# Token-major keys from matmuls, and two groups' queries on the two column halves of one bank

## The chip, the cores and the metric

The kernel runs on one core of one Trainium2 chip. The metric is the device time of one execution in microseconds (us); lower is better. The core has a matrix engine (TensorE; PE in the profile, with its weight loads as PEld), a vector engine (VectorE, DVE), a scalar engine (ScalarE, ACT), GpSimd (POOL) and SyncE (SP), which here only issues DMAs. Each engine works through its own list of instructions in order. Matmuls write to PSUM, a small memory in banks of 512 fp32 values a partition; the other engines read the results from there.

## The reference

Two stages follow each other for a batch of 8 sequences of 3200 tokens with 256 features:

```python
scores = (1.0 / S) * np.matmul(z, z.transpose(0, 2, 1))      # z: 8 x 3200 x 64
attn   = np.maximum(scores, 0.0) ** 2
x      = u * np.matmul(attn, v)                               # u, v: 8 x 3200 x 256
wq, wk = x @ w_q, x @ w_k                                     # 256 -> 64
W_tok  = (1.0 / np.sqrt(64)) * np.einsum('bsd,btd->bst', wq, wk)
mixed  = np.einsum('bst,btd->bsd', W_tok, x)
out    = np.maximum(mixed, 0.0) @ w_out                       # 256 -> 256
```

The second stage has no nonlinearity between `W_tok` and `x`, so the kernel never forms `W_tok`: it computes the 64x256 matrix wk^T x, here called the heads, and then wq times that.

## The kernel before, in words

**Tiling.** A sequence has 25 tiles of 128 tokens. Output tokens are worked on in seven groups: six of four tiles (512 tokens) and one of a single tile. For a group, the scores of a token tile against the group's tokens are a 64x512 matmul (line 291), whose contraction has only 64 rows. Two such matmuls go to the two 64-row halves of the array ("lanes") and run side by side. The first stage (lines 303 and 305, on ACT or DVE) takes relu and a scale from PSUM to SBUF, the second (lines 314 and 316, on ACT or POOL) squares to fp16, tile `at`. The second product (line 448) multiplies `at` with `v` into two accumulators of a bank each, `acc0` and `acc1`, also in two lanes of 64 rows: a first pass does one bank with rows 0 to 63 and the other with rows 64 to 127, a second pass swaps them (`first_pass`, line 385; `second_pass`, line 396; a wait in `swap_after`, line 427, stands between).

**Turned blocks.** The score matrix is symmetric. For some pairs of groups (`is_turned`, line 221) the block of one is not computed again: its `at` tile is transposed by a DMA into a `tt` tile (line 335) and used for the other group. Ten of the fifteen pairs of wide groups are turned.

**The second stage.** When a group is complete its accumulators are multiplied by `u` into `x` (`gate`, line 472), and a DMA transposes `x` to `xT` (line 502). `keys_and_heads` (line 797) then issues the projections: a matmul with stationary weights [w_q w_k] of 128 columns and moving `xT`, 512 tokens wide, gives queries and keys at once, features on partitions (line 508). ACT copies them to SBUF (line 528), and a DMA transposes the keys half to token-major (`turn_keys`, line 530, DMA at 535). The heads matmuls (line 545) of an earlier group stand in the other bank of the same PSUM tile. At the end of a batch the heads are turned on TensorE by two matmuls with all 128 rows (line 594); `mix` (line 636) multiplies them with the queries, `mix_out` takes relu, and `project` (line 788) multiplies with w_out and writes the result.

**Order.** The instruction order is fixed by the Python program: a loop of steps `k`, each with six score tiles (four with a mix), one stretch of the second product, and at most one extra piece of the second stage: keys ("k"), mix ("m") or projection ("p"). Which piece comes is decided by due times (`between`, `mix_due`, `key_due`) and, for some steps, by a table `chosen` (line 895). The two lanes of such a piece are balanced by the columns that their matmuls stream, and the items of both lanes are emitted in order of their place in the lane (`Streams`, line 368). The last batch's tail is a list written by hand (`ENDING`, line 82). SP issues the `tt`, `xT` and key transposes, the `u` loads and the output stores, in order; POOL issues the loads of `v` and `z`.

Of the kernel before, what the change touches and what calls it, by code (L numbers as in the profile page):

```python
# [16 lines left out]
def kernel(  # L17
# [15 lines left out]
    P = 128  # L33
# [23 lines left out]
    pk = ctx.enter_context(tc.tile_pool(name="pk", bufs=1))  # L57
# [7 lines left out]
    pq = ctx.enter_context(tc.tile_pool(name="pq", bufs=11))  # L65
# [24 lines left out]
    zT, vs, us, xs, xTs, qks, ks, hacc, hss, rts, zds = ({} for _ in range(11))  # L90
# [91 lines left out]
    wqk = consts.tile([P, ND, 2, dh], FP16, tag="wqk", name="wqk")  # L182
    wkq = consts.tile([P, ND, 2, dh], FP16, tag="wkq", name="wkq")
    hz = [consts.tile([P, D], FP16, tag=f"hz{i}", name=f"hz{i}") for i in range(2)]
    wq2 = consts.tile([P, ND, 2, dh], FP16, tag="wq2", name="wq2")
    wk2 = consts.tile([P, ND, 2, dh], FP32, tag="wk2", name="wk2")
    wo = consts.tile([P, ND, D], FP16, tag="wo", name="wo")
    zeros = consts.tile([P, P], FP16, tag="zeros", name="zeros")
    kxs = [pk.tile([P, 4, 2, dh], FP16, tag=f"kx{i}", name=f"kx{i}") for i in range(4)]
# [16 lines left out]
    def cast_weights():  # L206
        nc.gpsimd.tensor_copy(out=wqk[:, :, 0, :], in_=raw["q"])
        nc.gpsimd.tensor_copy(out=wqk[:, :, 1, :], in_=raw["k"])
        nc.gpsimd.tensor_copy(out=wkq[:, :, 1, :], in_=raw["q"])
        nc.gpsimd.tensor_copy(out=wkq[:, :, 0, :], in_=raw["k"])  # L210

    def double_weights(half):
        nc.gpsimd.tensor_copy(out=wq2[:, :, half, :], in_=raw["q"])
        nc.gpsimd.tensor_copy(out=wk2[:, :, half, :], in_=raw["k"])
# [5 lines left out]

    def is_turned(gi, gj):
        return gi < gj < LASTG and (gj <= gi + FAR or (gi, gj) == (0, 4))
# [46 lines left out]
    tt_of, tt_free = {}, [(-1.0, n) for n in range(7)]  # L269
# [77 lines left out]
    class Item:  # L347
# [4 lines left out]
        def emit(self, rows, start, stop):  # L352
            return nc.tensor.matmul(  # L353
                out=self.out, lhsT=self.lhsT(rows), rhs=self.rhs(rows), start=start, stop=stop
            )

# [151 lines left out]
    def projections(b, gi, w, out, start=True, n0=0, n1=None):  # L508

        n1 = widths[gi] // P if n1 is None else n1  # L510
        return [
            Item(
                out=out,
                lhsT=lambda r, ac=ac: w[r, ac, :, :].rearrange("p t h -> p (t h)"),
                rhs=lambda r, ac=ac: xTs[b, gi][r, n0:n1, ac, :],
                start=(start and ac == 0),
                stop=(ac == ND - 1),
            )
            for ac in range(ND)
        ]  # L520

    def projections_out(b, gi, out):
        gw = widths[gi]
        if gi < LASTG:
            qks[b, gi] = pq.tile([P, W], FP16, tag="qk", name="qk")
        else:
            qks[b, gi] = pq.tile([P, P], FP16, tag="ql", name="ql", bufs=2)
        nc.scalar.copy(out=qks[b, gi][:, 0:gw], in_=out)  # L528

    def turn_keys(b, gi):  # L530
        gw = widths[gi]
        mine = slice(0, dh) if swapped(gi) else slice(dh, P)
        kxs.append(kxs.pop(0))
        ks[b, gi] = kxs[-1]
        nc.sync.dma_start_transpose(
            out=ks[b, gi][:, 0 : gw // P, 0, :],
            in_=qks[b, gi][mine, 0:gw],
        )

    def swapped(gi):  # L540
        return gi % 2 == 1 or gi == LASTG

    def heads(b, gis, ps, stop=True):

        parts = [(gi, n) for gi in gis for n in range(widths[gi] // P)]
        if b < last:
            return [
                Item(  # L550
                    out=ps[:, 1, ds(P + cc * dh, dh)],
                    lhsT=lambda r, gi=gi, n=n, cc=cc: xs[b, gi][r, n, ds(cc * P, P)],
                    rhs=lambda r, gi=gi, n=n: ks[b, gi][r, n, 0, :],
# [8 lines left out]
                out=ps[:, 1, 0:D],  # L562
                lhsT=lambda r, gi=gi, n=n: ks[b, gi][r, n, :, :].rearrange("p a h -> p (a h)"),
# [7 lines left out]
    def heads_out(b, gis, ps):  # L571
        cols, n = (P, ND * dh) if b < last else (dh, D)
        part = ps[:, 1, P : P + n] if b < last else ps[0:dh, 1, 0:D]
        if gis[0] == 0:
            hacc[b] = psml.tile([P, n], FP32, tag="hT" if b < last else "ha", name="ha", bufs=1)
            nc.vector.tensor_copy(out=hacc[b][0:cols, :], in_=part)
        elif gis[-1] < LASTG:
            nc.vector.tensor_add(out=hacc[b][0:cols, :], in0=hacc[b][0:cols, :], in1=part)
        else:
            hT = psml.tile([P, ND, 2, dh], FP16, tag="h16", name="hT")  # L580
            for t in range(2):
                nc.vector.tensor_add(
                    out=hT[:, :, t, :],
                    in0=hacc[b][:].rearrange("p (a h) -> p a h", a=ND),
                    in1=part.rearrange("p (a h) -> p a h", a=ND),
                )
            hacc.pop(b)
            hTs[b] = hT


# [35 lines left out]
    def last_heads(b, g32, ps):  # L626
        for cc in range(ND):
            nc.tensor.matmul(  # L628
                out=ps[:, 1, 0:D],
                lhsT=wk2[:, cc, :, :].rearrange("p t h -> p (t h)"),  # L630
# [5 lines left out]
    def mix(b, pair, db):  # L636

        ps = ps_tile("mx")
        for a in range(2):
# [4 lines left out]
                rhs=qks[b, 2 * pair + a][half : half + dh, :],  # L644
# [19 lines left out]
    def last_mix(b, banks):  # L664
        rts[b, LASTG] = prt.tile([P, ND, P], FP16, tag="rs", name="rs", bufs=2)
        for db in range(ND):
# [4 lines left out]
                rhs=qks[b, LASTG][half : half + dh, 0:P],  # L671
# [62 lines left out]
    def side_mix(b, ps):  # L734
# [4 lines left out]
                rhs=lambda r: qks[b, LASTG][r, 0:P],  # L739
# [56 lines left out]

    def keys_and_heads(b, gis):

        ps = ps_tile("qk")
        outs = [ps[:, 0, 0:W], ps[:, 1, D : D + P]]  # L800
        w = wkq if swapped(gis[0]) else wqk
        banks = [projections(b, gis[0], w, outs[0]), []]
        aside = None
        late = len(groups) <= NG
        heads_of = keyed[: late or len(keyed) == 2]
        if late and len(keyed) == 2 and keyed[0][0] == keyed[1][0]:
            heads_of = [(keyed[0][0], keyed[0][1] + keyed[1][1])]
            keyed[:2] = heads_of
        full = len(heads_of) == 1
        if full:  # L810
            banks[1] += heads(*heads_of[0], ps, stop=(len(gis) == 1 and not side))
            if len(gis) > 1:
                banks[1] += projections(b, gis[1], w, outs[1], start=False)
            elif side:
                aside = side.pop(0)
                banks[1] += aside[0](aside[2], ps)
            more = sum(map(width, banks[1])) - ND * W // 2
            if heads_of[0][0] < last and more < D:

                outs[0] = ps[:].rearrange("p a w -> p (a w)")[:, P : P + W]
                banks[0] = projections(b, gis[0], w, ps[:, 0, P:W], n1=W // P - 1)
                banks[1][-1].stop = False
                banks[1] += projections(b, gis[0], w, ps[:, 1, 0:P], start=False, n0=W // P - 1)
        assert full or len(gis) == 1
        if full and heads_of[0][0] < last and heads_of[0][1][-1] == LASTG:
            assert not aside and len(gis) == 1
            hb_ = heads_of[0][0]
            to_turn_heads.append(lambda: turn_heads(hb_, hTs.pop(hb_), ps))  # L830

        def after():
            for gi, o in zip(gis, outs):
                projections_out(b, gi, o)
                turn_keys(b, gi)
            if full:
                hb, hgis = keyed.pop(0)
                heads_out(hb, hgis, ps)
                if hgis[-1] == LASTG:
                    mixed_at[0] = max(mixed_at[0], now[0] - 1)  # L840
                    todo_mix.extend((hb, i, db) for i in range(LASTG // 2) for db in range(ND))
                    side.append((side_mix, side_mix_out, hb))
            if aside:
                aside[1](aside[2], ps)
            keyed.append((b, gis))
            keyed_at[0] = now[0]

        return banks, after

    def group_begun(k, b, gi):  # L850
# [24 lines left out]
    first_kx = list(kxs)  # L875
# [7 lines left out]
    due(11, lambda: clear(zr[:, NT, :], first_kx[0][:]))  # L883
    due(12, lambda: double_weights(0))
    due(14, lambda: double_weights(1))
    due(15, lambda: clear(*[t[:] for t in first_kx[1:]], *[t[0:dh, :] for t in hz]))
# [7 lines left out]
    heading_more = {165: -1}  # L894
    chosen = {
        18: "k", 19: "p", 20: "p", 21: "m", 35: "k", 36: "p", 38: "p", 101: "p", 142: "mp",
        147: "k", 148: "m", 149: "m", 159: "mp", 161: "p", 163: "m"
    }
# [342 lines left out]
    def ending(order):  # L1241
        for word in order.split():
            what, n, more = word[0], int(word[1:2] or 0), word[2:]
            if what == "H":
                ps_["hd"] = ps_tile("hd")
                heads_ = heads(last, sum((kgis for _, kgis in keyed), []), ps_["hd"], stop=False)
                for fn in whole([heads_]):
                    fn()
# [9 lines left out]
            elif what == "q":  # L1258
                gi = LASTG - 1 + n
                o = home("qq", more)[0][:, 0 : widths[gi]]  # L1260
                for fn in whole([projections(last, gi, wq2, o)]):
                    fn()
                projections_out(last, gi, o)
# [74 lines left out]
```

## Time and profile before

| | |
|---|---|
| time, median of 3 runs | 765.44 us (765.44 to 765.54) |
| profiled execution | 765.27 us |
| its span, first to last instruction | 763.5 us |
| matmuls recorded | 12888 |
| granted TensorE clock, mean | 0.997 |

"Busy" is the union of an engine's instruction times. Matmuls overlap: a 64-row matmul of 256 columns is recorded with 269 ns, but the next one on the same rows starts well before it ends, so starts and not durations say what a matmul's place costs. In the rows of the timeline the columns are the start in us, the length of the stretch in us, the engine, the line, the operation, the tiles (output<-inputs), the shape of the array that is used (rows*columns) and the size of the operand that streams, with a count. In the rows of groups, after the bar, stand the busy time in us, the mean of one in ns, and the idle time before them with what ended it. In the rows of waits stand the total in us, the number of waits and the longest. Line 353 is a helper that emits nearly all matmuls, so those are told apart by their tiles.

### The profile page before, as it was taken

How to read it: one execution, taken by the hardware profiler on the slowest of the kernel's cores; microseconds unless marked ns; L12 is line 12 of the kernel's file. 1: busy time of each engine (PE TensorE's matmuls, PEld its weight loads, DVE VectorE, ACT ScalarE, POOL GpSimd, SP SyncE). 2: the span in 40 equal slices, each digit the busy share in tenths (PEclk: the TensorE clock that was granted, in tenths of full speed). 3: DMA queues.
4: the chain of work that ended last, by engine and by line, in shares of the span. 5: the costliest groups of instructions: out<-in, count | busy, mean ns of one | idle time of the engine just before them, and what ended most of it. 6: DMA issues, size and time to landing. Idle time of an engine off the chain costs nothing.

```text
span 763.5 us, 28995 instructions
## 1 busy us (share of the span) xinstructions
PE 753.3 (99%) x12888; PEld 617.9 (81%) x12888; DVE 462.0 (61%) x458; ACT 526.4 (69%) x619; POOL 545.3 (71%) x383
## 2 busy tenths in 40 slices
PE   8999999999999999999999999999999999999996
PEld 6777888888888887888888888888878888888884
DVE  7654676546755567555665557655566565755534
ACT  8666676676767676676775867658676586776555
POOL 7988797678867688675888569966698665854540
PEclk9999999999999999999999999999999999999998
DMA  9999699997999979999999979999599995798636
GB/s 193 176 191 201 104 175 175 141 181 112 183 172 205 188 146 187 201 189 171 191 195 194 210 151 150 169 201 237 105 198 204 200 209 127 170 227 188 168 74 261
DMA packets 289613, 135.88 MB, mean 178 GB/s; under 512 B 265168, under 2 KB 269648, under 8 KB 289488
## 3 DMA queue, kind: packets, MB, share of 16 engines
q1 hardware_dynamic: 279696, 117.80, 80.2%
q0 software_dynamic: 9648, 15.98, 15.3%
q8 instruction: 100, 1.64, 0.9%
q14 instruction: 25, 0.20, 0.1%
q10 hardware_dynamic: 144, 0.26, 0.1%
HBM read 59.38 MB, written 26.21 MB: 112 GB/s over the span
## 4 chain that ended last, share of the span: by engine, by line
PE 97%; DVE 2%; ACT 1%; issue 0%; DVEq 0%; ACTq 0%
PE acc L353 72%; PE sc L291 12%; PE fo L353 5%; PE qk L353 5%; PE mx L641 1%; DVE x_sb L491 1%; DVE fo L1296 0%; PE sc L965 0%; DVE g L305 0%; ACT at L314 0%; ACT g L303 0%; PE qk L594 0%; PE xtx L618 0%; PE ztp L129 0%; PE hd L628 0%
## 5 line engine op out<-in xcount | busy, mean ns | idle before, releaser
L305 DVE TENSOR_SCALAR g<-sc 128x1024 f32<-128x1024 f32 x329 | 400.6, 1224 | 240.2 <-PE sc L291 228.5
L316 POOL TENSOR_TENSOR at<-g 128x1024 f16<-128x1024 f32 x229 | 432.3, 1897 | 123.9 <-DVE g L305 100.2
L353 PE MATMUL acc<-v_sb,at 64*128 64x256 f16 (+1 forms) x7187 | 462.0, 269 | 2.2 <-DVE x_sb L491 0.5
L353 PEld LDWEIGHTS <-at 64*128 64x128 f16 (+1 forms) x7187 | 353.9, 94 | 87.6 <-PE acc L353 25.3
L314 ACT ACTIVATE at<-g 128x1024 f16<-128x1024 f32 x227 | 236.2, 1055 | 19.3 <-DVE g L305 11.8
L353 PE MATMUL acc<-v_sb,tt 64*128 64x256 f16 x2552 | 178.7, 269 | 0.0
L303 ACT ACTIVATE g<-sc 128x1024 f32<-128x1024 f32 x127 | 130.0, 1023 | 55.3 <-PE sc L291 52.3
L291 PE MATMUL sc<-zT 64*128 64x512 f16 (+1 forms) x1008 | 164.7, 356 | 0.4 <-DVE zT L135 0.3
L353 PEld LDWEIGHTS <-tt 64*128 64x128 f16 x2552 | 130.2, 94 | 14.1
L493 POOL TENSOR_TENSOR x_sb<-gt,u_sb 128x512 f16<-128x512 f32 x48 | 61.2, 1274 | 64.5 <-ACT gt L490 60.1
L662 ACT ACTIVATE rt<-mx 128x1024 f16<-128x1024 f32 x47 | 47.9, 1024 | 32.7 <-PE mx L641 32.5
L490 ACT COPY gt<-acc 128x512 f32<-128x512 f32 x48 | 28.1, 585 | 49.9 <-PE acc L353 49.9
L291 PEld LDWEIGHTS <-zT 64*128 64x128 f16 x1008 | 51.8, 94 | 8.7 <-issue 1.5
L353 PE MATMUL fo<-wo,rt 64*128 64x256 f16 (+1 forms) x696 | 57.9, 270 | 0.0
L528 ACT CAST qk<-qk 128x512 f16<-128x512 f32 x47 | 27.5, 586 | 39.5 <-PE qk L353 36.9
L353 PEld LDWEIGHTS <-rt 64*128 64x128 f16 (+1 forms) x696 | 35.5, 94 | 15.3 <-PE fo L353 6.3
L491 DVE TENSOR_TENSOR x_sb<-acc,u_sb 128x512 f16<-128x512 f32 x48 | 33.2, 691 | 20.4 <-PE acc L353 19.2
L723 ACT ACTIVATE fo<-fo 128x1024 f32<-128x1024 f32 x39 | 39.9, 1024 | 1.9 <-PE fo L353 1.7
L353 PEld LDWEIGHTS <-x_sb 64*128 64x128 f16 x672 | 29.8, 95 | 4.5 <-PE qk L353 0.9
L353 PE MATMUL qk<-kx,x_sb 64*128 64x64 f16 x672 | 32.8, 190 | 0.0
L146 POOL DMA_DIRECT2D v_sb<-in_v_dram x49 | 28.7, 586 | 0.0
L353 PE MATMUL qk<-xT_sb,wkq 64*128 64x512 f16 (+3 forms) x118 | 25.7, 326 | 0.0
(84 smaller groups left out, 249.8 us busy)
## 6 DMA issues: line engine op xcount, KB each, us to landing
u_sb<-in_u_dram SPq DMA_DIRECT2D x48, 512.0 KB, 5.4
out_dram<-fo SPq DMA_DIRECT2D x43, 512.0 KB, 3.9
v_sb<-in_v_dram POOLq DMA_DIRECT2D x43, 256.0 KB, 5.2
tt<-at SPq DMA_TRANSPOSE x162, 5.1
out_dram<-fo SPq DMA_DIRECT2D x9, 256.0 KB, 2.9
zr<-in_z_dram POOLq DMA_DIRECT2D x7, 256.0 KB, 4.2
u_sb<-in_u_dram SPq DMA_DIRECT2D x8, 128.0 KB, 4.4
zr<-in_z_dram POOLq DMA_DIRECT2D x7, 144.0 KB, 6.4
```

Source lines behind the costliest of these rows:

```text
L146: nc.gpsimd.dma_start(out=vs[b][:, n0 : n0 + nn, :], in_=rows(v, b)[:, n0 : n0 + nn, :])
L291: nc.tensor.matmul(out=sc[:, h, at : at + w], lhsT=zT[b][half : half + dqk, ds(z_at(b, h) + ti * P, P)], rhs=zT[b][half : half + dqk, ds(z ...
L303: nc.scalar.activation(out=g[:], in_=sc[:], func=RELU, scale=GSCALE)
L305: nc.vector.tensor_scalar(out=g[:], in0=sc[:], scalar1=0.0, scalar2=GSCALE, op0=AOP.max, op1=AOP.mult)
L314: nc.scalar.square(out=out, in_=g[:])
L316: nc.gpsimd.tensor_mul(out=out, in0=g[:], in1=g[:])
L353: return nc.tensor.matmul(out=self.out, lhsT=self.lhsT(rows), rhs=self.rhs(rows), start=start, stop=stop)
L490: nc.scalar.copy(out=upper[:], in_=accs[1][:])
L491: nc.vector.tensor_mul(out=x[:, 0:n], in0=accs[0][:, 0:n], in1=ug[:, 0:n])
L493: nc.gpsimd.tensor_mul(out=x[:, n : 2 * n], in0=upper[:], in1=ug[:, n : 2 * n])
L662: nc.scalar.activation(out=out, in_=ps[:], func=RELU)
L723: nc.scalar.mul(out=flat_out[:, sl], in_=part, mul=FINAL_SCALE)
```

## The change

- Keys are computed token-major on TensorE: the stationary operand is a tile of `xT` (128 tokens as columns) and the moving one is w_k, 64 columns wide (`key_items`). DVE copies eight tiles of keys from one bank to SBUF (`kk`). The DMA transposes of the keys go, and so do the cleared buffers for them.
- Queries come by themselves. The two groups of a pair share one bank: group a has stationary w_q, 64 columns, and writes partitions 64a to 64a+63, so that each matmul uses 64 rows and 64 columns of the array (`queries_and_keys`, `Both`). One ACT copy takes both groups' queries. For each such pair, keys stand in the other bank and lane.
- Heads get calls of their own (`heads_call`), three a batch, in a PSUM tile `hd`, with the seventh group's queries and keys beside them. The last batch's heads use 64 columns of the array in place of doubled keys.
- Three more score blocks are turned: (0,3), (1,4) and (2,5) beside (0,4). Eleven `tt` buffers stand in place of seven; the query buffers are six in place of eleven.
- Due times follow, and the table `chosen` has entries for steps 129 to 151 alone.

```diff
-    pq = ctx.enter_context(tc.tile_pool(name="pq", bufs=11))
+    pq = ctx.enter_context(tc.tile_pool(name="pq", bufs=6))
...
+    ALSO = ((0, 3), (0, 4), (1, 4), (2, 5))
+
     def is_turned(gi, gj):
-        return gi < gj < LASTG and (gj <= gi + FAR or (gi, gj) == (0, 4))
+        return gi < gj < LASTG and (gj <= gi + FAR or (gi, gj) in ALSO)
...
+    class Both:
+        def __init__(self, one, two):
+            self.one, self.two, self.out = one, two, one.out
+            self.start, self.stop = one.start, one.stop
+
+        def emit(self, rows, start, stop):
+            self.one.emit(rows, start, stop)
+            return self.two.emit(rows, start, stop)
...
+    def queries(b, gi, out, half=None):
+        cols = slice(0, 2) if half is None else slice(half, half + 1)
+        return [
+            Item(
+                out=out,
+                lhsT=lambda r, ac=ac: wq2[r, ac, cols, :].rearrange("p t h -> p (t h)"),
+                rhs=lambda r, ac=ac: xTs[b, gi][r, 0 : widths[gi] // P, ac, :],
...
-    def turn_keys(b, gi):
...
+    def key_items(b, parts, out, start=True):
+        return [
+            Item(
+                out=out[:, ds(i * dh, dh)],
+                lhsT=lambda r, gi=gi, n=n, ac=ac: xTs[b, gi][r, n, ac, :],
+                rhs=lambda r, ac=ac: wk1[r, ac, :],
...
+    def queries_and_keys(b, pair):
+        gis = [2 * pair, 2 * pair + 1]
+        ps = ps_tile("qk")
+        banks = [
+            [
+                Both(*two)
+                for two in zip(*(queries(b, gi, ps[ds(a * dh, dh), 0, :], a) for a, gi in enumerate(gis)))
+            ],
+            key_items(b, tiles_of(gis), ps[:, 1, :]),
+        ]
+
+        def after():
+            qqs[b, pair] = pq.tile([P, W], FP16, tag="qk", name="qk")
+            nc.scalar.copy(out=qqs[b, pair][:], in_=ps[:, 0, :])
+            kks[b, pair] = pk.tile([P, 8, dh], FP16, tag="kk", name="kk")
+            nc.vector.tensor_copy(
+                out=kks[b, pair][:].rearrange("p n h -> p (n h)"), in_=ps[:, 1, :]
+            )
...
     def group_done(k, b, gi):
-        if gi < LASTG - 1:
-            between(k + (5 if b + 1 < B else 3), lambda: keys_and_heads(b, [gi]))
-        elif gi == LASTG and b + 1 < B:
-            between(k + 5, lambda: keys_and_heads(b, [LASTG - 1, LASTG]))
+        if gi < LASTG - 1 + (b < last) and gi % 2 == 1:
+            between(k + (4 if b < last else 3), lambda: queries_and_keys(b, gi // 2))
+        elif gi == LASTG - 2 and b == last:
+            between(k + 3, lambda: one_query_and_keys(b, gi))
+        elif gi == LASTG and b < last:
+            between(k + 4, lambda: heads_call(b, small=True))
```

More of the change, by code (lines that the diff above doesn't have):

```diff
@@ L206, in cast_weights @@
     def cast_weights():
[L207 to L214, printed above, removed]
+        for half in range(2):
+            nc.gpsimd.tensor_copy(out=wq2[:, :, half, :], in_=raw["q"])
+        nc.gpsimd.tensor_copy(out=wk1[:], in_=raw["k"])
+        nc.gpsimd.tensor_copy(out=wk32[:], in_=raw["k"])
     def cast_out_weights():
@@ new lines, in tiles_of, with queries_out @@
+    def tiles_of(gis):
+        return [(gi, n) for gi in gis for n in range(widths[gi] // P)]
+    def queries_out(b, gi, src):
+        if gi == LASTG:
+            qss[b] = pq.tile([P, P], FP16, tag="ql", name="ql", bufs=2)
+            nc.scalar.copy(out=qss[b][:], in_=src)
+            return
+        if (b, gi // 2) not in qqs:
+            qqs[b, gi // 2] = pq.tile([P, W], FP16, tag="qk", name="qk")
+        mine = slice(gi % 2 * dh, gi % 2 * dh + dh)
+        nc.scalar.copy(out=qqs[b, gi // 2][mine, :], in_=src[mine, :])
@@ new lines, in one_query_and_keys, with after @@
+    def one_query_and_keys(b, gi):
+        ps = ps_tile("qk")
+        n = widths[gi] // P
+        banks = [queries(b, gi, ps[:, 0, :]), key_items(b, tiles_of([gi]), ps[:, 1, 0 : n * dh])]
+        aside = side.pop(0) if side else None
+        if aside:
+            banks[1][-1].stop = False
+            more = aside[0](aside[2], ps)
+            more[0].start = False
+            banks[1] += more
+        def after():
+            if aside:
+                aside[1](aside[2], ps)
+            queries_out(b, gi, ps[:, 0, :])
+            kks[b, gi // 2] = pk.tile([P, 8, dh], FP16, tag="kk", name="kk")
+            nc.vector.tensor_copy(
+                out=kks[b, gi // 2][:, 0:n, :].rearrange("p n h -> p (n h)"),
+                in_=ps[:, 1, 0 : n * dh],
+            )
+            keyed.append((b, [gi]))
+            keyed_at[0] = now[0]
+        return banks, after
@@ L548, in heads, with keys @@
+    def keys(b, gi, n):
+        return kss[b][:] if gi == LASTG else kks[b, gi // 2][:, gi % 2 * 4 + n, :]
+    def heads(b, parts, out, stop=True):
         if b < last:
@@ L569, in heads, with heads_call, after @@
         ]
[L571 to L574, printed above, removed]
-            hacc[b] = psml.tile([P, n], FP32, tag="hT" if b < last else "ha", name="ha", bufs=1)
[L576 to L579, printed above, removed]
+    def heads_call(b, small=False):
+        hb, gis = keyed.pop(0)
+        assert hb == b
+        final = b < last and gis[0] == LASTG - 2
+        if final:
+            gis = gis + [LASTG]
+        ps = ps_tile("hd")
+        parts = tiles_of(gis)
+        outs = [ps[:, i, 0:P] if b < last else ps[0:dh, i, 0:D] for i in range(2)]
+        one = ND * dh if b < last else D
+        aside = side.pop(0) if side and not final else None
+        more = [[], []]
+        if small:
+            more[0] += queries(b, LASTG, ps[:, 0, P : 2 * P])
+            more[1] += key_items(b, [(LASTG, 0)], ps[:, 1, P : P + dh])
+        if aside:
+            more[1] += aside[0](aside[2], ps)
+        for i in more[0] + more[1]:
+            i.start = False
+        wide = [sum(map(width, m)) for m in more]
+        cut = round((len(parts) * one + wide[1] - wide[0]) / (2 * one))
+        banks = [heads(b, parts[:cut], outs[0]), heads(b, parts[cut:], outs[1])]
+        for bank, m in zip(banks, more):
+            if m:
+                for i in bank + m:
+                    i.stop = False
+                if b < last:
+                    m[-1].stop = True
+                    bank += m
+                else:
+                    bank[0].start, m[0].start, m[-1].stop = False, True, True
+                    bank[:] = m[:1] + bank + m[1:]
+        if final:
+            to_turn_heads.append(lambda: turn_heads(b, hTs.pop(b), ps))
+        def after():
+            heads_out(b, outs, gis[0] == 0, final)
+            if small:
+                queries_out(b, LASTG, ps[:, 0, P : 2 * P])
+                kss[b] = pk.tile([P, dh], FP16, tag="ks", name="ks", bufs=2)
+                nc.vector.tensor_copy(out=kss[b][:], in_=ps[:, 1, P : P + dh])
+                between(now[0] + 2, lambda: heads_call(b))
+            if aside:
+                aside[1](aside[2], ps)
+            if final:
+                mixed_at[0] = max(mixed_at[0], now[0] - 1)
+                todo_mix.extend((b, i, db) for i in range(LASTG // 2) for db in range(ND))
+                side.append((side_mix, side_mix_out, b))
+            keyed_at[0] = now[0]
+        return banks, after
@@ new lines, in heads_out @@
+    def heads_out(b, parts, first, final):
+        if first:
+            rows_, n = (P, ND * dh) if b < last else (dh, D)
+            hacc[b] = psml.tile([P, n], FP32, tag="hT" if b < last else "ha", name="ha", bufs=1)
+            nc.vector.tensor_copy(out=hacc[b][0:rows_, :], in_=parts[0])
+        rows_ = P if b < last else dh
+        acc = hacc[b][0:rows_, :]
+        for part in parts[int(first) : 1 if final else 2]:
+            nc.vector.tensor_add(out=acc, in0=acc, in1=part)
+        if final:
@@ L795, in project @@
         )
[L797 to L848, printed above, removed]
     def group_begun(k, b, gi):
@@ L874 @@
     last = B - 1
-    first_kx = list(kxs)
     now = [0]
@@ L1260, in ending @@
                 o = home("qq", more)[0][:, 0 : widths[gi]]
-                for fn in whole([projections(last, gi, wq2, o)]):
+                for fn in whole([queries(last, gi, o)]):
                     fn()
-                projections_out(last, gi, o)
+                queries_out(last, gi, o)
             elif what == "m":
```

83 lines of the change are left out of this document (31 added, 52 removed).

## The prediction

> **What bounds the kernel now.** I read the page's engine totals and chain first, then the stretches of the span, then the groups of instructions with their shapes, and at last TensorE's own timeline around the places that the change touches.
>
> ```profile
> span 763.5 us, 28995 instructions
> PE 753.3 (99%) x12888; PEld 617.9 (81%) x12888; DVE 462.0 (61%) x458; ACT 526.4 (69%) x619; POOL 545.3 (71%) x383
> ...
> PE 97%; DVE 2%; ACT 1%; issue 0%; DVEq 0%; ACTq 0%
> PE acc L353 72%; PE sc L291 12%; PE fo L353 5%; PE qk L353 5%; PE mx L641 1%; DVE x_sb L491 1%; DVE fo L1296 0%; PE sc L965 0%; DVE g L305 0%; ACT at L314 0%; ACT g L303 0%; PE qk L594 0%; PE xtx L618 0%; PE ztp L129 0%; PE hd L628 0%
> ```
>
> ```profile
> core 0: us, PE busy (x) PEld busy (x) DVE busy (x) ACT busy (x) POOL busy (x), PEclk, DMA share, GB/s
> ...
> 24.00:740.00 716.00, 714.41 (x12482) 589.51 (x12480) 434.47 (x424) 495.51 (x581) 525.52 (x361) 1.00 0.98 177
> ```
>
> TensorE makes 97% of the chain that ended last, and between 24 and 740 us it is busy 714.41 of 716.00 us at the full granted clock. The other three engines have a quarter of their time or more free there. So the time is what TensorE's stream takes: a matmul less shortens the run by its place in the stream, and a hole in the stream lengthens it. The DMA share of 0.98 is a sum of packet times, and no link of the chain is a DMA; I come back to it.
>
> What a matmul's place costs is read from starts, not from durations, since two matmuls on the two halves of the array's rows run side by side:
>
> ```profile
> 353.58 1.04 PE L353 MATMUL acc<-v_sb,at 64*128 64x256 f16 x16
> 354.46 0.19 PE L353 MATMUL qk<-kx,x_sb 64*128 64x64 f16 x1
> 354.46 0.38 PE L353 MATMUL qk<-xT_sb,wkq 64*128 64x512 f16 x1
> 354.49 0.36 PE L353 MATMUL qk<-kx,x_sb 64*128 64x64 f16 x7
> 354.68 0.38 PE L353 MATMUL qk<-xT_sb,wkq 64*128 64x512 f16 x1
> 354.69 0.38 PE L353 MATMUL qk<-wo,rs 64*128 64x256 f16 x2
> 354.89 0.61 PE L353 MATMUL acc<-v_sb,tt 64*128 64x256 f16 x8
> ```
>
> Here a 64x512 projection occupies one half of the rows from 354.46 to 354.68, 0.22 us, while eight 64x64 heads matmuls pass through the other half in the same 0.22 us, 27.5 ns each. All have the tile 64*128: 64 rows, 128 columns. The second kind of evidence is what happens when the tile changes:
>
> ```profile
> 327.71 1.04 PE L353 MATMUL acc<-v_sb,tt 64*128 64x256 f16 x16
> 328.68 0.28 PE L594 MATMUL qk<-ident,hT 128*128 128x128 f16 x2
> 328.90 0.39 PE L641 MATMUL mx<-qk,hs 64*128 64x512 f16 x2
> 329.12 0.38 PE L291 MATMUL sc<-zT 64*128 64x512 f16 x2
> 329.34 0.49 PE L353 MATMUL acc<-v_sb,at 64*128 64x256 f16 x6
> ```
>
> Sixteen acc matmuls take 0.88 us of stream (353.58 to 354.46 above), so those that start at 327.71 are through at 328.59; the 128*128 pair starts only at 328.68, 0.09 us later. It needs 2 x 0.055 us (128 columns are a quarter of the 0.22 us of 512), to 328.79, and the next 64*128 matmul starts at 328.90, 0.11 us later. No such hole stands between mx, sc and acc, whose tile is the same: 0.22 us each. So a change of tile empties the array, about 0.1 us each time, and nothing of the one tile runs beside the other.
>
> **The change part by part.** Durations are from this profiled execution: 765.27 us, of which 763.5 are the span and 1.8 lie around it; the median of the runs shown, 765.44, is 0.2 us above.
>
> ```profile
> L305 DVE TENSOR_SCALAR g<-sc 128x1024 f32<-128x1024 f32 x329 | 400.6, 1224 | 240.2 <-PE sc L291 228.5 <-POOL at L316 3.2 <-ACT g L303 2.3
> ...
> L291 PE MATMUL sc<-zT 64*128 64x512 f16 x880 | 159.5, 376 | 0.4 <-DVE zT L135 0.3
> ...
> L353 PE MATMUL qk<-kx,x_sb 64*128 64x64 f16 x672 | 32.8, 190 | 0.0
> ...
> L491 DVE TENSOR_TENSOR x_sb<-acc,u_sb 128x512 f16<-128x512 f32 x48 | 33.2, 691 | 20.4 <-PE acc L353 19.2 <-DMA u_sb<-in_u_dram 0.5
> ...
> L528 ACT CAST qk<-qk 128x512 f16<-128x512 f32 x47 | 27.5, 586 | 39.5 <-PE qk L353 36.9 <-PE mx L641 2.6
> ```
>
> *Three more blocks turned.* In each of 8 batches 3 blocks of 4 token tiles are no longer scored: 96 of the 880 sc matmuls go, 48 pairs, each 0.22 us of stream (328.90 to 329.34 holds two): **-10.6 us**. The second product reads a turned tile where it read a scored one, with the same matmuls. The 48 first stages (1224 ns on DVE) and second stages that go lie on engines beside TensorE: nil.
>
> *Queries and keys, columns alone.* Before, two groups take 8 projections of 64x512 for each row half: with 2 halves and 2 lanes 4 x 0.22 = 0.88 us, heads apart. After, one pass of a pair holds, on one row half, two pairs of query matmuls 64x512, each pair on the two column halves (tile 64*64), and on the other row half 16 key matmuls of 64 columns. If the pair shares its 0.22 us, that is 0.44 us against 16 x 27.5 ns = 0.44 us, twice for the two row halves: 0.88 us. The saving on the queries is spent on the keys: nil. The heads stay 700 matmuls of 64 columns, in calls of their own: nil. Whether two matmuls on the same rows and different columns share their time is shown by no row; one place of 0.22 us or two are the bounds, and the nearest row, mx with its two matmuls on different rows in 0.22 us, says one. I take one.
>
> *The tile changes.* The instruction order of the changed kernel has, in each pass, a pair of 64*64 queries, eight 64*128 keys, a pair of queries, eight keys, between 64*128 acc matmuls. That is 4 changes of tile, in 44 passes (176 query matmuls, 4 a pass). Before, the program had 40 changes, all between 128 and 64 rows, and none inside a projection. What a change of columns alone costs no row shows. The bounds are nothing and full emptying, a gain is excluded since the order of TensorE is kept; the nearest row is the change of rows above, so I take it: 0.10 us, the mean of 0.09 and 0.11. The larger part is then that queries and keys no longer overlap: a pass is 4 x 0.10 + 2 x 0.22 + 16 x 0.0275 = 1.28 us, where it would be 0.44. 44 x 0.84 = **+37.0 us**. The last batch's heads (4 changes) and a few 128*64 tiles at the end (2 more changes than before, net) add 6 x 0.10 = 0.6 us: **+37.6** in all.
>
> The Trainium skill, "TensorEngine Tiling (Array Packing)", section Tiling Modes, Key Properties, says that changing the tiling mode, not just the tile, drains TensorE. By that rule all 180 new changes drain and the sum is the one above; this trace agrees where rows change, with 0.09 and 0.11 us, and shows no change of columns.
>
> *Waits.* TensorE waits on itself where lanes change banks:
>
> ```profile
> PEld L353 <- PE acc L353: 25.3, 106, 0.3
> ...
> ACT at L314 <- DMA tt<-at: 5.1, 4, 2.7
> ...
> POOL at L316 <- DMA tt<-at: 3.8, 4, 1.3
> ```
>
> The loop's last step has number 152 in place of 167, counted by the kernel's own bookkeeping, so perhaps a tenth of the 25.3 us goes: at most -2.5, and as the extra calls are as many as before I count none. The keys' new copy on DVE, 128x512 from PSUM, is bounded by the 586 ns of L528 and the 691 ns of L491: 24 of them, 17 us, covered by 30 first stages fewer on DVE (37 us). It is read two steps (some 9 us) later. ACT loses half its L528 casts. Were that cover gone, a copy would delay a heads call by under 0.7 us, 16 us over 24 pairs.
>
> *DMA.*
>
> ```profile
> q1 hardware_dynamic: 279696, 117.80, 80.2%
> ...
> tt<-at SPq DMA_TRANSPOSE x162, 5.1
> ...
> kx<-qk SPq DMA_TRANSPOSE x47, 4.3
> ...
> kx<-ql SPq DMA_TRANSPOSE x7, 3.8
> ```
>
> SP issues 48 more tt transposes of 128x1024 (0.262 MB) and 54 key transposes fewer (64x512, 0.066 MB, and 7 small): +9.4 MB. Queue q1 needs 612 us of packet time for 117.80 MB, so +49 us: 661 of a span of 790.5, 84%. The moves past SP's queue are six fewer issues in all. The turned blocks are read a group or more later, so late ones show as at buffers not given back: 8.9 us on ACT and POOL for 162 now, 2.6 for 48 more, none on TensorE. Nil, with 0 to 2.6 us as bounds. POOL's fewer casts and clears in the opening: nil, behind the z loads.
>
> Sum: 763.5 - 10.6 + 37.6 = 790.5, and 1.8 around it: **792.3 us**.
>
> **The rivals.**
>
> *A change of columns does not empty the array.* Then queries and keys overlap as the projection and the heads do at 354.46, and only the saving stays: 763.5 - 10.6 + 1.8 = **754.7**, faster. For it: nothing in the trace changes columns, and every hole seen goes with rows that both tiles need. Against it: after the last 128*128 matmul the hole comes though its rows are free in order. The place is the 44 passes, and it decides when a pass takes less than 0.44 + 10.6/44 = 0.68 us. The Trainium skill, "TensorE: Matmul & The Clock Gate", Part 3, tells of row and column tiles packed in one array and running concurrently, 2.38 times faster for three column tiles; no run here shows it, and it speaks for the shared 0.22 us more than against a drain between unlike tiles.
>
> *Only the row half that changes empties.* Queries drain in and out on their half, keys go on: 2 x 0.10 x 44 = 8.8 us, **763.5**, a hair faster.
>
> *Side by side does not happen*, so that the change does not do what it says: each query pair takes 0.44. Without emptying the passes last 0.88: 44 x 0.44 = 19.4, **774.1**; with it, 792.3 + 19.4 = **811.7**.
>
> *The DMA becomes the bound*: the 0.98 speaks for it, TensorE's full 714 of 716 us beside it against it; 2.6 us at most by the rows above, inside the others' ranges.
>
> **How the numbers follow.** Emptying with a shared place: 0.66 (with its size open: half the hole takes 9 us off, and holes half as long again add as much: 783 to 801). Emptying and no sharing 0.05; no emptying 0.18; half the array 0.07; no emptying, no sharing 0.04. What a measurement of this kernel can tell from no change is about 0.2%. Slower: 0.66 + 0.05 + 0.04 = 0.75; the half-array case, 0.25% faster by its sum, is split: faster 0.18 + 0.04 = 0.22, same 0.03. The range reaches from 755, in the middle of the no-emptying case, to 803; it leaves out 811.7, half of 0.18 and the main case's tail, under 0.2. The likeliest case's own range is 783 to 801.
>
> **What would show it.** Right: in the timeline of the new kernel a qk stretch of about 1.28 us a pass, with a query pair (64*64) starting some 0.1 us after the last key has streamed and the keys after the queries' 0.22 us, not beside them; sc 784 matmuls; tt transposes 210; TensorE still about all of the chain; DVE, ACT and POOL less busy in us. Wrong: keys and queries starting within 10 ns of each other, passes of 0.44 us and a span near 753; query pairs 0.22 us apart on the same rows would mean that they do not share; waits of PEld on DMA tt or of ACT and POOL on it well over 10 us would mean that the transposes bind.

## The result, and the profile after

The changed kernel takes 813.33 us (median of 4 runs, 810.33 to 815.90) against 765.48 us before: a ratio of 1.062, 95% interval 1.0585 to 1.0662. It is slower, as forecast, but by 47.9 us where 26.9 were forecast, and above the range. The profiled execution is the fastest of the four, 810.33 us, with a span of 808.4. The four runs lie 5.6 us apart, where those of before lie within 0.1: a part of the new time differs from run to run, so differences of 2 or 3 us between this kernel and its variants are not read. In the sets of runs further down the kernel before took 765.4 to 765.9 us. Ratios leave out a run that is over 1.5% longer than the fastest of its kernel, so a ratio can differ from the quotient of two medians.

The page of the changed kernel, totals and chain:

```profile
span 808.4 us, 29903 instructions
PE 786.4 (97%) x13426; PEld 631.1 (78%) x13426; DVE 440.9 (55%) x458; ACT 473.4 (59%) x554; POOL 496.7 (61%) x351
...
PE 89%; DVE 3%; ACT 3%; DMA 3%; issue 2%; SPq 0%; ACTq 0%; DVEq 0%
PE acc L349 64%; PE sc L287 9%; PE qk L349 7%; PE fo L349 5%; DMA tt<-at 2%; PE hd L349 2%; DVE g L301 1%; PE mx L750 1%; ACT at L310 1%; DVE x_sb L496 1%; ACT g L299 1%; DVE fo L1347 0%; SPq L331 0%; DMA z<-in_z_dram 0%; ACT fo L832 0%
```

TensorE still carries most of the chain, 89% where it was 97%; DVE, ACT and POOL have less work than before (441, 473 and 497 us where it was 462, 526 and 545). So the scores that went did relieve them, and no gain from that is to be seen. Here are a pass of queries and keys and the end of the next one, from TensorE's timeline of the changed kernel:

```profile
305.30 0.59 PE L287 MATMUL sc<-zT 64*128 64x512 f16 x4
305.96 0.40 PE L349 MATMUL qk<-xT_sb,wq 64*64 64x512 f16 x2
306.29 0.40 PE L349 MATMUL qk<-wk,xT_sb 64*128 64x64 f16 x8
306.62 0.40 PE L349 MATMUL qk<-xT_sb,wq 64*64 64x512 f16 x2
306.96 0.40 PE L349 MATMUL qk<-wk,xT_sb 64*128 64x64 f16 x8
...
308.97 0.32 PE L349 MATMUL qk<-wk,xT_sb 64*128 64x64 f16 x5
309.10 0.28 PE L349 MATMUL acc<-v_sb,at 64*128 64x256 f16 x1
```

The two queries of a row go together (one row, x2, 0.40 us in all, no longer than one such matmul): side by side works. But the keys start only 0.33 us after the queries (305.96 to 306.29), 0.12 more than the 0.21 to 0.22 us that 512 columns stream, and the next queries 0.33 us after the first key. Nothing of the keys runs beside the queries, though they use the other half of the rows. At 309.10 the acc matmul, which has the keys' tile, starts while keys still run. In the rows of waits the emptying has no releaser that could be named, so it falls under "issue", with other idle time that has none:

```profile
PEld L349 <- issue: 38.8, 138, 2.4
...
POOL at L312 <- DMA tt<-at: 17.6, 9, 3.8
...
ACT at L310 <- DMA tt<-at: 13.0, 5, 6.1
```

The same "issue" wait was 5.7 us in 19 times before, and the waits of POOL and ACT on turned blocks 3.8 and 5.1 us: together 30.6 us where they were 8.9. That is well over the 10 us that the prediction gave as a sign that the transposes bind, so the experiments have to settle it.

From the starts of all matmuls, with a stream of 512 columns counted as 0.213 us, I worked out when the array is empty (sums over all holes of the span; the first and last microseconds, outside the matmuls, left out):

| us | before | after | difference |
|---|---|---|---|
| empty, at a change of tile | 4.8 (40 holes) | 25.2 (221 holes) | +20.4 |
| empty, at other places | 11.4 | 26.1 | +14.7 |
| streaming in one or both lanes | 739.5 | 748.6 | +9.1 |

The streaming is 48 pairs of sc fewer, -10.6, and 44 passes in which queries (0.43 us) and keys (0.46 us) follow each other where 0.44 would do, +19.7: together +9.1. So the passes cost 20.4 + 19.7 = 40.1 us, the saved scores bring 10.6, and 14.7 us are holes elsewhere. The three lines of the table make 44.2 of the 44.9 us between the two spans.

The holes elsewhere are mostly a few long ones. Seven of them, 0.87 to 2.47 us each, make 9.8 of the 26.1 us; before, the longest was 0.50 us. TensorE's rows of waits in the changed kernel name what ended them; four of these rows:

```profile
PE acc L349 <- ACT at L310: 2.8, 2, 2.3
PE acc L349 <- issue: 2.2, 1, 2.2
...
PE sc L287 <- ACT zT L172: 1.2, 1, 1.2
...
PE hd L349 <- ACT fo L832: 0.9, 1, 0.9
```

Six of the seven end when ACT has finished a piece: `at`, `zT`, `g`, `fo` twice and `fs`. The longest is the one with `at`, at 49 us: there ACT itself had waited 6.15 us for the DMA that turns a block. The seventh, 2.35 us at 367 us, has no releaser that the profile could name.

### The profile page after: what moved, and what is told of

It reads as the page before. It is cut to its first block, busy times and chain, and to the rows that moved or that the text cites. A ratio compares the mean times of both kernels' runs of the same rounds, so it can differ in the third digit from the quotient of the medians.

```text
span 808.4 us, 29903 instructions
## 1 busy us (share of the span) xinstructions
PE 786.4 (97%) x13426; PEld 631.1 (78%) x13426; DVE 440.9 (55%) x458; ACT 473.4 (59%) x554; POOL 496.7 (61%) x351
## 4 chain that ended last, share of the span: by engine, by line
PE 89%; DVE 3%; ACT 3%; DMA 3%; issue 2%; SPq 0%; ACTq 0%; DVEq 0%
PE acc L349 64%; PE sc L287 9%; PE qk L349 7%; PE fo L349 5%; DMA tt<-at 2%; PE hd L349 2%; DVE g L301 1%; PE mx L750 1%; ACT at L310 1%; DVE x_sb L496 1%; ACT g L299 1%; DVE fo L1347 0%; SPq L331 0%; DMA z<-in_z_dram 0%; ACT fo L832 0%
## 5 line engine op out<-in xcount | busy, mean ns | idle before, releaser
L301 DVE TENSOR_SCALAR g<-sc 128x1024 f32<-128x1024 f32 x299 | 363.8, 1223 | 277.5 <-PE sc L287 256.7
L312 POOL TENSOR_TENSOR at<-g 128x1024 f16<-128x1024 f32 x205 | 386.8, 1895 | 167.0 <-DVE g L301 105.3
L349 PE MATMUL acc<-v_sb,at 64*128 64x256 f16 (+1 forms) x6411 | 420.9, 269 | 4.6 <-ACT at L310 2.8
L349 PEld LDWEIGHTS <-at 64*128 64x128 f16 (+1 forms) x6411 | 318.3, 94 | 76.3 <-PE acc L349 24.2
L310 ACT ACTIVATE at<-g 128x1024 f16<-128x1024 f32 x203 | 211.0, 1054 | 26.3 <-DMA tt<-at 13.0
L349 PE MATMUL acc<-v_sb,tt 64*128 64x256 f16 (+1 forms) x3296 | 214.4, 269 | 2.2 <-issue 2.2
L349 PEld LDWEIGHTS <-tt 64*128 64x128 f16 (+1 forms) x3296 | 166.6, 94 | 19.9 <-issue 2.6
L287 PEld LDWEIGHTS <-zT 64*128 64x128 f16 x912 | 49.4, 94 | 11.4 <-issue 4.8
L349 PEld LDWEIGHTS <-rt 64*128 64x128 f16 (+1 forms) x696 | 37.0, 94 | 14.7 <-PE fo L349 5.6
L349 PEld LDWEIGHTS <-xT_sb 64*128 64x128 f16 (+1 forms) x728 | 27.4, 95 | 22.0 <-issue 20.4
L349 PE MATMUL qk<-wk,xT_sb 64*128 64x64 f16 (+1 forms) x728 | 40.2, 191 | 0.1
L349 PE MATMUL qk<-xT_sb,wq 64*64 64x512 f16 (+2 forms) x182 | 36.7, 399 | 0.1
```

The source lines that it names most:

```text
L287: nc.tensor.matmul(out=sc[:, h, at : at + w], lhsT=zT[b][half : half + dqk, ds(z_at(b, h) + ti * P, P)], rhs=zT[b][half : half + dqk, ds(z ...
L301: nc.vector.tensor_scalar(out=g[:], in0=sc[:], scalar1=0.0, scalar2=GSCALE, op0=AOP.max, op1=AOP.mult)
L310: nc.scalar.square(out=out, in_=g[:])
L312: nc.gpsimd.tensor_mul(out=out, in0=g[:], in1=g[:])
L349: return nc.tensor.matmul(out=self.out, lhsT=self.lhsT(rows), rhs=self.rhs(rows), start=start, stop=stop)
```

## The experiments

Two theories stood against each other. T: changes of tile empty the array and part queries from keys, so the passes carry most of the loss. D: the loss is DMA, blocks turned too late, and the passes are no bound. All ratios are against the kernel before, run on the same chip in the same set.

**No tile of 64 columns.** The weights are padded with zeros to 128 columns and the two groups accumulate in the one bank (a cut, its lines set closer than in the kernel):

```diff
-                Both(*two)
-                for two in zip(*(queries(b, gi, ps[ds(a * dh, dh), 0, :], a) for a, gi in enumerate(gis)))
+                Item(out=ps[:, 0, :], lhsT=lambda r, ac=ac, a=a: wqz[r, ac, a, :, :].rearrange("p t h -> p (t h)"),
+                     rhs=lambda r, ac=ac, gi=gi: xTs[b, gi][r, 0 : widths[gi] // P, ac, :],
+                     start=(a == 0 and ac == 0), stop=(a == 1 and ac == ND - 1))
+                for a, gi in enumerate(gis) for ac in range(ND)
```

> The changed kernel with its queries in full-width tiles: the weights of group a are [w_q, 0] or [0, w_q], 128 columns, and the four query matmuls of a pass accumulate in the one bank. No tile of 64 columns is left in the passes. Theory T (changes of tile empty the array and part queries from keys): a pass takes four places of 0.22 us with the keys beside them, 0.88 us, where the changed kernel's trace shows about 1.36; 44 x 0.48 = 21 us less, about 792. Rival D (the time was lost to DMA-turned blocks that come late, and the passes are no bound): the time stays at 810 to 816.

Measured: 786.79 us, 1.030 (1.0246 to 1.0359), 26.5 us less than the changed kernel. The queries no longer share a place, so they take twice as many, and the kernel is faster. Its timeline shows the keys beside the queries again, and acc matmuls moving into the lane that the keys leave free:

```profile
301.00 0.37 PE L352 MATMUL qk<-xT_sb,wqz 64*128 64x512 f16 x1
301.00 0.39 PE L352 MATMUL qk<-wk,xT_sb 64*128 64x64 f16 x8
...
301.27 0.38 PE L352 MATMUL acc<-v_sb,at 64*128 64x256 f16 x2
301.43 0.38 PE L352 MATMUL qk<-xT_sb,wqz 64*128 64x512 f16 x1
```

By the count above the profiled execution is 19.6 us shorter at changes of tile and 7.5 in streaming, since a pass doesn't keep both lanes for 0.88 us, and 3.7 longer in other holes. The gain itself, 26.5 us, is not clearly more than the 21 expected: the two intervals leave about 5 us open.

**All queries of a pass ahead of its keys.** Two changes of tile a pass in place of four:

```diff
+        for i in banks[0]:
+            i.ahead = True
```

`Streams.add` is changed with it: an item that is so marked takes the place of the first of its run.

> The changed kernel with all four query matmuls of a pass ahead of its 16 keys: two changes of tile a pass in place of four, all else the same. Theory T: 88 changes fewer at 0.11 us, 10 us less, about 803.5. Rival D: no difference, 810 to 816.

Measured: 803.92 us, 1.049 (1.0466 to 1.0521): 9.4 us less, for 88 changes fewer. So one change costs 0.11 us; the count of holes gives the same, 25.2 us at 221 changes and 15.2 at 133.

**Keys in 64x64 as well.** One tile for the whole pass; each key matmul becomes two:

```diff
...
+                Item(out=out[ds(c * dh, dh), :], lhsT=lambda r, c=c: lhsT(r)[:, ds(c * dh, dh)], rhs=rhs)
+                for c in range(2)
...
```

> The changed kernel with each key matmul as two of 64x64 (tokens 0 to 63 and 64 to 127 on the two column halves), so that a whole pass has one tile and queries and keys may overlap again. Theory T, two changes a pass, and a bound from what a 64x64 key costs: if the two halves share their 27 ns, a pass takes 0.22 + 0.46 = 0.68 us, 30 us less, about 783; if each half takes 29 ns of its own, 0.22 + 0.93 = 1.15 us, 9 us less, about 804. If unlike tiles did overlap before and the holes have another cause, no gain. Rival D: 810 to 816.

Measured: 789.36 us, 1.031 (1.027 to 1.0347), 24 us less, where 30 were expected if the halves share and 9 if they don't. The timeline of the second pass of a call:

```profile
305.42 0.22 PE L349 MATMUL qk<-wk,xT_sb 64*64 64x64 f16 x2
305.42 0.40 PE L349 MATMUL qk<-xT_sb,wq 64*64 64x512 f16 x2
305.47 0.39 PE L349 MATMUL qk<-wk,xT_sb 64*64 64x64 f16 x14
305.66 0.38 PE L349 MATMUL qk<-xT_sb,wq 64*64 64x512 f16 x2
305.69 0.42 PE L349 MATMUL qk<-wk,xT_sb 64*64 64x64 f16 x16
306.04 4.34 PE L349 MATMUL acc<-v_sb,at 64*128 64x256 f16 x72
```

Queries and keys start together, and 32 key halves and four queries are through in 0.62 us with the emptying ahead of acc counted: the two column halves share most of their time, as the first case of the expectation had it, and only the changes in and out of the pass are left. The same products that waited for each other in the changed kernel overlap as soon as their tiles are alike. With the first two experiments this settles T against D for the passes. None of the three is faster than the kernel before.

**The ten blocks of before.** `ALSO = ((0, 4),)`: the three further blocks of each batch are scored again. The table of steps has three other entries.

> The changed kernel with only the ten blocks turned that were turned before (three blocks a batch scored again, 48 sc pairs at 0.22 us = 10.6 us more on TensorE; the table of steps at the end is another). Theory T says nothing on the holes outside the passes, of which the changed kernel has 14.7 us more than the kernel before. If the turned blocks' DMAs cause them (rival D for this part): 813.3 + 10.6 - 14.7 = about 809. If they come from elsewhere (the order of steps, the calls of heads): about 824.

Measured: 823.38 us, 1.075 (1.0736 to 1.0768): 10.1 us more, about what the 48 sc pairs cost. The sum of the holes outside the passes hardly changes, 24.9 us by the count above against 26.1, though POOL and ACT wait 12.6 us on turned blocks in place of 30.6. So the turned blocks are worth their price here, and they do not make most of these holes. That the other table moved the time as well is not excluded; what a table can be worth is measured further down.

**The keys alone.** The first experiment's weights and the fourth's blocks together: what is left of the change are token-major keys and heads in calls of their own, with the order of steps that goes with them.

> The changed kernel without column tiles (as the first experiment) and with only the ten blocks of before turned: token-major keys from matmuls and heads in calls of their own, nothing else of the change. By sums of the runs so far: 823.4 - 26.5 (what leaving out the column tiles brought) = 797. If the gain of leaving them out depends on the turned blocks, it lies nearer 813 or 787. Beside the kernel before, what is over 9.4 us (the queries' matmuls no longer shared with the keys') is holes.

Measured: 795.61 us, 1.040 (1.0362 to 1.0429), as the sum of the two said. Of its 30 us, 10.4 are matmul columns: a count of all matmuls' columns by half rows, at 0.213 us for 512, gives 732.9 us of stream where the kernel before has 722.5. Some 18 are holes (34.4 in place of 16.2). So this part by itself costs about as much as the column tiles.

**No stores.** The condition `if b == last:` ahead of the output DMA leaves out the output of the first seven batches' wide groups.

> The changed kernel that stores only the last batch's wide groups: the output of the other seven batches' wide groups is left out (21 MB less of 145 on the DMA engines). If late DMAs make the holes of about 2 us that stand outside the passes in the changed kernel's trace, they go, and the time falls by 5 to 8 us, to 805 to 808, with less spread. If not, it stays at 810 to 816.

Measured: 812.3 us, 1.059 (1.0557 to 1.0628). The medians lie 1 us apart, which is within the spread: the volume on the DMA engines is not what holds the changed kernel. With the fourth experiment this rules D out for most of the loss. A small part stays with it: without the stores POOL and ACT wait 16.7 us on turned blocks in place of 30.6, and the holes at other places are 23.5 us in place of 26.1.

**More turned blocks in the kernel before.** Three more blocks in six batches, 18 in all, or in seven, 21 in all; without the new keys, and with other entries in the table of steps. `MORE` is ((0, 3), (1, 4), (2, 5)):

```diff
-        return gi < gj < LASTG and (gj <= gi + FAR or (gi, gj) == (0, 4))
+        return gi < gj < LASTG and (
+            gj <= gi + FAR or (gi, gj) == (0, 4) or b < 6 and (gi, gj) in MORE
+        )
...
-    tt_of, tt_free = {}, [(-1.0, n) for n in range(7)]
+    tt_of, tt_free = {}, [(-1.0, n) for n in range(10)]
```

> The kernel before with the three further blocks a batch turned in six of its eight batches (18 blocks, 36 more DMA transposes; ten buffers for them in place of seven, other entries in the table of steps). Keys still come from the shared projection, turned by DMA; no tile of 64 columns. If turning is worth what the scores cost (72 sc matmuls fewer, 36 pairs at 0.22 us): 765.4 - 7.9 = 757.5, faster. If the further DMAs or the table of steps take it back: 765 or more.

> The same as the first kernel of this set, in seven of eight batches (21 blocks, 84 sc matmuls fewer, 42 pairs): 765.4 - 9.2 = 756.2 if nothing else follows. If the DMA queue is near its end, less than the 18 blocks bring.

Measured: 806.65 us, 1.051 (1.0448 to 1.0563), with 18 blocks, and 804.95 us, 1.051 (1.0464 to 1.0555), with 21: by the ratio some 39 us slower in both, where 8 to 9 us less would follow from the scores alone. The chain and two waits of the first of them:

```profile
PE 63%; DMA 16%; SPq 5%; POOL 5%; ACT 4%; issue 3%; DVE 3%; ACTq 0%; POOLq 0%; DVEq 0%
```

```profile
POOL at L320 <- DMA tt<-at: 123.0, 30, 9.9
...
ACT at L318 <- DMA tt<-at: 59.1, 26, 7.3
```

Here ACT and POOL wait 182 us for `at` buffers that a late turn still reads, where it was 9 before, and TensorE falls to 63% of the chain. What I had called hidden is hidden for the ten blocks a batch of before, 162 `tt` transposes, and no longer for 198. The table of steps is another too, and its share of the 39 us was not measured apart. Three further runs asked what the turns collide with:

> The kernel before with 18 further blocks turned, as in the fifth experiment, with the stores of the first seven batches' wide groups left out (that output is not written; 21 MB less on the DMA engines). If the volume on the DMA engines made the 41 us, the time falls by most of it, to 757 to 770. If the DMA engines have room and it is the chain of turns on SP's queue, the buffers or the table of steps, it stays near 800.

> The same kernel with 18 further blocks turned, stores kept, and the key transposes of the first seven batches left out (the keys there are zeros, so the result is not the reference's): 48 DMA issues and 2.9 MB less. By volume alone 2% of 145 MB would bring at most a few us: about 795 to 805. If the key transposes, in order on SP's queue among the others, are what the further ones collide with, the time falls to 757 to 775.

> The kernel before, its own table and its ten blocks, with the key transposes of the first seven batches left out (the keys there are zeros). It measures what these 48 transposes cost in the kernel before: if they are hidden, 764 to 766, and the change had nothing to gain from leaving them out except room for more turned blocks; if SP's queue is a limit already, 755 to 762.

Without the stores, 781.75 us, 1.021 (1.0191 to 1.0235); without the key transposes of seven batches (`if b == last:` ahead of the DMA in `turn_keys`), 787.37 us, 1.028 (1.0253 to 1.0304). Neither of the first two expectations was met: by the ratios 22 and 17 of the 39 us go. The key transposes are 2% of the bytes, so it isn't volume alone; the stores help too, so it isn't the key transposes alone. In the kernel before itself the same transposes can be left out for 765.00 us, 0.9986 (0.9977 to 0.9996): there they are hidden but for about 1 us.

**Another table of steps, kernel before.** `chosen = {144: 'mp'}` and `heading_more = {}`.

> The kernel before with another table of steps (one entry in place of the fifteen, and none for the heading): nothing else is changed. It says how much of the time hangs on the order of steps alone: the holes outside the passes, 16 us in the kernel before and 34 in the kernel with keys alone, should grow if the order makes them, to 770 to 785; if not, 765 to 767.

Measured: 774.15 us, 1.011 (1.0092 to 1.0136). The order of steps alone is worth 8.5 us. By the count above its holes at other places are 19.4 us, against 11.4, and most of the difference lies in the second tenth of the run and in the ninth. So the order makes holes, as the first of the two expectations had it. They are not the holes of the changed kernel, though: the four longest, 5.4 us, all end with matmuls of the heads, two of them after a wait for keys turned by DMA, which the changed kernel doesn't have.

## Why the prediction was right and wrong, step by step

The changed kernel's 47.9 us, as the runs part them (each from the one ahead of it): token-major keys, heads in calls of their own and the order that goes with them +30.2 (765.4 to 795.6), three more blocks a batch with their table -8.8 (795.6 to 786.8), queries on column halves +26.5 (786.8 to 813.3).

- **The bound.** Right in the main: TensorE makes 89% of the chain after the change, and the relief of the other three engines shows no gain. Its share was 97% before; that it fell fits the holes that the forecast left out, below.
- **The scores, -10.6.** Right: 10.1 in the changed kernel (fourth experiment) and 8.8 without column tiles, each with another table of steps beside it.
- **Sharing of the column halves.** Right: one place of 0.22 us, the two queries in one row of the timeline.
- **The tile changes, +37.6 with the last heads'.** The mechanism was right, and the extrapolation from a change of rows to one of columns held. The size was a little low: 40.1 by the trace. A change into 64*64 takes 0.09 us and one out of it 0.12 (medians of 90 each), and a key 29 ns, where I took 0.10 and 27.5. The Trainium skill, "TensorEngine Tiling (Array Packing)", Tiling Modes, Key Properties, says that changing the tiling mode drains TensorE. The trace agrees: there are holes at 221 changes of tile, 0.114 us on the average, and 180 of them are changes into or out of 64*64.
- **Queries and keys, columns alone: nil.** This held: by a count of the columns on each half of the rows the new keys take 10.4 us more, and the shared places of the queries take 9.4 less. With the column tiles off the 10.4 stand alone, as in the experiment on the keys.
- **Heads in calls of their own: nil; waits: none counted.** This is the step that failed. The forecast balanced columns and put the holes that a new order of pieces makes at nothing; of the waits it looked at one, TensorE's on its own accumulators, and that one did stay (25.3 us before, 24.5 after). The holes at other places grew by 14.7 us, almost exactly what the forecast lacks beside the 2.5 us of the passes: 790.5 + 2.5 + 14.7 = 807.7 of a span of 808.4. About half of the 14.7, 7.5 us, are six waits for pieces that ACT finishes later than TensorE needs them. Without column tiles and with ten blocks the same pieces make 18 us of holes, and another table alone makes 8 us in the kernel before. So a new order can make holes of this size; that it made these is likely and not shown.
- **The DMA, nil, 0 to 2.6 us.** Right within the spread for the time of the changed kernel (1 us without the stores), wrong for the waits: 21.7 us more on POOL and ACT where 2.6 were taken, and one hole of 2.5 us on TensorE behind them. The price, so many waits for each turned block, took the waits as proportional; in the kernel before they grew from 9 to 182 us with 18 more blocks, and the time by some 39 us. That the changed kernel bears more turned blocks because its keys are no longer transposed would fit the 17 us that leaving out the key transposes brought there; no run put them back into the changed kernel.
- **The rivals.** No emptying is excluded by the timeline. Emptying and no sharing gave 811.7, close to the measured time, but its mechanism did not happen: that the number fits is chance. The half-array case is excluded too, since keys on the other rows wait.

What stays open: which calls of the new order make the 14.7 us of holes. Their places are known (of 20.3 us in holes over 20 ns at other places, 7.0 lie in the first tenth of the span and 3.7 in the ninth), and what ended the seven longest stands above but for one; with other tables for the changed kernel it might be less, and none was tried. Nor is it settled how the 39 us of the turned blocks in the kernel before part between queue order, buffers, volume and the table of steps.

## What to carry to other kernels

Before packing matmuls on column or row tiles, count how often the stream changes its tile shape: here each change cost 0.11 us and, worse, kept apart what two lanes would have run together, so that queries that need half the places cost 26.5 us more. If a small tile is used, use it for everything in that stretch, or put all of it together. A balance of columns says nothing of holes: in a kernel whose order has been fitted, run the old kernel with another order to see how much may hang on it, 8.5 us here. And a queue that hides 162 transposes need not hide 36 more at the same price each.

## What the runs showed of the hardware

- Matmuls in the two 64-row lanes overlapped here only when their tiles had the same shape: 64*64 queries and 64*128 keys followed each other 0.33 us apart, and both in 64*64 started together. Changing the columns from 128 to 64 and back empties the array just as changing the rows does: 0.09 to 0.12 us.
- Pairs of 64x64 matmuls on the two column halves of the same rows, each with its own weights, went through at 16 ns a matmul on the average in the third experiment, where single 64*128 ones that stream the same 64 columns took 29 in the changed kernel.
- Leaving out the key transposes of seven batches, 2.9 MB, brought some 17 us in the kernel with 198 `tt` transposes and 1 us in the one with 162.
